# A pair of linear attentions on one core: the places of all jobs written anew

## The chip, the cores and the metric

The kernel runs on one core of a Trainium2 chip. The metric is the time of one execution on the device in microseconds (us). The core has five engines, each with its own stream of instructions, which it works off strictly in order: TensorE (PE, matmuls), VectorE (DVE), ScalarE (ACT), GpSimd (POOL) and SyncE (SP). SP and POOL also issue the DMA transfers, each on a queue of its own (q1 hardware for SP, q0 software for POOL). Engines wait for each other on semaphores.

## The reference, cut to what matters

```python
def _A_ref(x, wqkv, wo):                   # x [1, 2048, 640], wqkv [640, 1920], wo [640, 640]
    qkv = (x @ wqkv).reshape(B, S, 3, 32, 20)       # then q, k, v per head
    phi = lambda t: jnp.where(t > 0, t + 1, jnp.exp(t)) + 1e-6
    pq, pk = phi(q), phi(k)
    kv  = jnp.einsum("bhsd,bhse->bhde", pk, v)
    z   = jnp.einsum("bhsd->bhd", pk)
    num = jnp.einsum("bhqd,bhde->bhqe", pq, kv)
    den = jnp.einsum("bhqd,bhd->bhq", pq, z)[..., None] + 1e-6
    return (num / den) [heads joined] @ wo
```

There are two such blocks, A and B, each with an x and weights of its own, and the results are put side by side. All is float32.

## The kernel before, in words

**Arithmetic.** Each float32 operand is split into a high part (rounded to the format that TensorE takes, written by ACT) and a low part (source less high part, by DVE), and each product is made of three matmuls, high by high, high by low, low by high. In the names of tiles, `h` and `l` at the end are the two parts. The products with wk, wq and the output matrix use a scheme with seven products in place of eight (`STEPS`, `product`), which needs sums and differences of quarter tiles of x: for pair p of 128-row tiles, `A1`, `A2`, `A5` are pieces of x (tiles `kah`, `kal`) and `S1`, `S3` the sums (`sx`, rounded to `ksh`, `ksl`). Seven products of a pair are called n = 0 to 6; between them ACT copies partial results out of PSUM (`c0` after product 0, `c2` after 2, `c4` after 4, `c5` after 5), and DVE adds others (`q3`, `q4`, `q6`). Products 2, 4 and 5 use again the PSUM bank that c0, c2, c4 empty, so they can't start before these copies are done.

**The k half** (from the start to about 285 us): for both inputs, tile by tile, pk = phi(x wk), then G = pk^T x, and from G with wv the state kv. Tile n of 32 (16 per input) gives `xt` (transposed tile, for the products), `xn` (plain tile, for G; split by `nh` on ACT, L484, and `nl` on DVE), `ek`, `ko`, `pkh`, `pkl` (phi and its two parts: jobs `exp`, `relu`, `mix`, `ph`, `pl`), and a store `zs` that adds phi to an accumulator in DRAM. The tiles are in groups of four, i = 0 to 7; a group's products of two pairs come first, with the sums of G (`psg`) of the group before between them.

**The form of x from the k half.** The low parts and the sums that the k half makes of the last groups' x are stored to DRAM (`xd` by SP, jobs `st`; `sd` by POOL, jobs `ss`, for pairs 10 to 13, two sums S1 and S3 with a high and a low part each) and loaded again for q.

**The q half** (from about 285 us): per block of 512 rows u, pq = phi(x wq), its denominator, the division, and the output with a matrix that holds kv and wo. The last two blocks (6 and 7, the "joint q") are computed together with the seven-product scheme on the forms of x that the k half stored (`qpair`, slots `r` 0 to 45): `load_xs` loads plain x (512-byte runs), `xs_lo` and `x5_lo` load low parts from `xd`, `load_s` loads sums from `sd`. Meanwhile block 5 finishes: four `gather` DMAs (`rd<-da`) bring 1/denominator, DVE divides (L1036), ACT and DVE split the result. Then come three output blocks (`outmm`), whose products also wait for copies out of PSUM (`o<-pa`, `o<-pe`).

**What sets the order.** Nothing is scheduled by a tool: the order of every engine's stream is the order in which the program issues it. In the k half, PE's work is a list of steps, and all other work is a list of jobs, each at a float place near a step. Three tables at the top of the file shift them: `MOVED` shifts steps, `SHIFT` shifts jobs (`SHIFT.get(name, 0)` is added to the job's place), and the sorted list is then issued. In the q half jobs hang at slots of `line`, one per matmul group, and `AT` moves a job by so many slots:

```python
spot = round((place[spot] if isinstance(spot, tuple) else spot) + SHIFT.get(name, 0), 2)   # job
steps.sort(key=lambda w: w[0] + MOVED.get(w[2], 0))                                        # arrange
slot = line[line.index(slot) + AT.get((f.__name__,) + a, 0)]                               # at
```

Since each engine works in order, a job that waits holds up all that stands behind it on the same engine. SP and POOL too: an issue that waits for a buffer or for data holds up the issues behind it. Buffers come from pools with a fixed number per tag (the tiles `xt` and `xn` share five, the sums have two), so the order also decides which buffer a tile gets and what it must wait for.

## Time and profile before

| | |
|---|---|
| median of three runs | 570.23 us (570.09 to 571.23) |
| the profiled execution | 570.55 us, span 568.8 us |
| PE | 560.7 us busy (99%), 3219 instructions |
| DVE | 432.4 us (76%), 739 |
| ACT | 335.4 us (59%), 627 |
| POOL | 102.5 us (18%), 167 |
| DMA | 136.19 MB, mean 239 GB/s; q1 (SP) 48.6% and q0 (POOL) 29.1% of 16 engines' span |

A row of a timeline gives start, length, engine, line, operation, output and inputs, and in brackets the idle time before it with what ended it. `<-` stands between output and inputs; buffer numbers are left out. A row of the windows gives the stretch, its length, then the busy time and count of PE, of PE's weight loads, DVE, ACT and POOL, then the granted clock of PE (1.00 is full), the share of the 16 DMA engines that was busy, and GB/s. A matmul's start follows that of the one ahead in 0.15 us (320 columns) or 0.23 us (512 columns), though each row is 0.31 or 0.39 us long, since they are pipelined.

### The profile page before, as it was taken

How to read it: one execution, taken by the hardware profiler on the slowest of the kernel's cores; microseconds unless marked ns; L12 is line 12 of the kernel's file. 1: busy time of each engine (PE TensorE's matmuls, PEld its weight loads, DVE VectorE, ACT ScalarE, POOL GpSimd, SP SyncE). 2: the span in 40 equal slices, each digit the busy share in tenths (PEclk: the TensorE clock that was granted, in tenths of full speed). 3: DMA queues.
4: the chain of work that ended last, by engine and by line, in shares of the span. 5: the costliest groups of instructions: out<-in, count | busy, mean ns of one | idle time of the engine just before them, and what ended most of it. 6: DMA issues, size and time to landing. Idle time of an engine off the chain costs nothing.

```text
span 568.8 us, 9177 instructions
## 1 busy us (share of the span) xinstructions
PE 560.7 (99%) x3219; PEld 511.1 (90%) x3219; DVE 432.4 (76%) x739; ACT 335.4 (59%) x627; POOL 102.5 (18%) x167
## 2 busy tenths in 40 slices
PE   9999999999999989999999999999999999999997
PEld 7989999898989978989888899898989989779997
DVE  5889798886585867878754896968969496769881
ACT  5874667662775856565835774645537273574441
POOL 0111122311014323243010103111012211100110
PEclk9999999999999999999999999999999999999999
DMA  8869789999898897999997995847567897940322
GB/s 262 245 163 247 182 234 312 270 322 355 296 249 233 209 303 139 355 280 235 317 323 266 324 308 171 283 142 248 168 227 243 276 369 226 321 155 20 112 94 92
DMA packets 85174, 136.19 MB, mean 239 GB/s; under 512 B 10312, under 2 KB 45512, under 8 KB 85128
## 3 DMA queue, kind: packets, MB, share of 16 engines
q1 hardware_dynamic: 70600, 88.90, 48.6%
q0 software_dynamic: 14240, 46.48, 29.1%
q8 instruction: 25, 0.41, 0.3%
q10 hardware_dynamic: 288, 0.23, 0.1%
q14 instruction: 21, 0.17, 0.1%
HBM read 78.34 MB, written 54.09 MB: 233 GB/s over the span
## 4 chain that ended last, share of the span: by engine, by line
PE 91%; DMA 3%; DVE 2%; ACT 2%; issue 1%; SPq 0%; DVEq 0%; ACTq 0%
PE pa L337 20%; PE pe L337 10%; PE psg L163 8%; PE psg L164 8%; PE psg L162 8%; PE psb L337 7%; PE psq L162 6%; PE psq L164 6%; PE psq L163 6%; PE psk L605 5%; DMA xn<-in_B_x 2%; PE pskv L787 2%; PE pa L1230 1%; DMA x<-xd 1%; DMA x<-in_B_xt 1%; PE pe L1230 1%
## 5 line engine op out<-in xcount | busy, mean ns | idle before, releaser
L162 PE MATMUL psg<-pkh,xnh 128*128 128x512 f32 x160 | 62.7, 392 | 0.0
L164 PE MATMUL psg<-pkh,xnl 128*128 128x512 f32 x160 | 62.7, 392 | 0.0
L163 PE MATMUL psg<-pkl,xnh 128*128 128x512 f32 x160 | 62.6, 392 | 0.0
L162 PE MATMUL psq<-xqh,wqh 128*128 128x512 f32 x150 | 58.9, 393 | 0.0
L164 PE MATMUL psq<-xqh,wql 128*128 128x512 f32 x150 | 58.5, 390 | 0.0
L163 PE MATMUL psq<-xql,wqh 128*128 128x512 f32 x150 | 58.4, 390 | 0.0
L341 ACT ACTIVATE o<-pa 128x320 f32<-128x320 f32 x64 | 27.7, 437 | 51.7 <-PE pa L337 51.6
L572 POOL DMA_DIRECT2D zd<-ek x30 | 26.3, 876 | 125.7 <-DVE ek L564 44.8
L341 ACT ACTIVATE ko<-pa 128x320 f32<-128x320 f32 x52 | 22.4, 434 | 38.9 <-PE pa L337 38.6
L164 PEld LDWEIGHTS psg<-pkh,xnl 128*128 128x128 f32 x160 | 30.0, 188 | 6.5
L163 PEld LDWEIGHTS psg<-pkl,xnh 128*128 128x128 f32 x160 | 30.1, 188 | 5.5 <-DVE pkl L580 0.3
L162 PEld LDWEIGHTS psg<-pkh,xnh 128*128 128x128 f32 x160 | 30.1, 188 | 5.2
L1036 DVE SCALAR_TENSOR_TENSOR pq<-pq,rd 128x1280 f32<-128x1280 f32 x16 | 23.1, 1480 | 13.9 <-DMA rd<-da 13.9
L164 PEld LDWEIGHTS psq<-xqh,wql 128*128 128x128 f32 x150 | 28.2, 188 | 6.0
L163 PEld LDWEIGHTS psq<-xql,wqh 128*128 128x128 f32 x150 | 28.2, 188 | 5.4
L162 PEld LDWEIGHTS psq<-xqh,wqh 128*128 128x128 f32 x150 | 28.2, 188 | 5.4
L576 ACT ACTIVATE pkh<-ek,epst 128x640 fp32r<-128x640 f32 x32 | 25.9, 823 | 10.7 <-DVE ek L564 10.6
L650 DVE TENSOR_TENSOR gacc<-psg,gacc 128x512 f32<-128x512 f32 (+2 forms) x42 | 25.6, 628 | 8.5 <-PE psg L164 8.4
L564 DVE SCALAR_TENSOR_TENSOR ek<-ek,ko 128x640 f32<-128x640 f32 x32 | 26.2, 820 | 6.3 <-ACT ko L561 4.0
L155 ACT ACTIVATE dah<-pq 128x1024 fp32r<-128x1024 f32 (+2 forms) x24 | 17.7, 773 | 22.6 <-DVE pq L1036 22.6
L433 ACT ACTIVATE ksh<-sx 128x512 fp32r<-128x512 f32 x26 | 16.3, 629 | 24.6 <-DVE sx L451 24.5
L580 DVE SCALAR_TENSOR_TENSOR pkl<-ek,pkh 128x640 fp32r<-128x640 f32 x32 | 25.9, 820 | 5.6 <-ACT pkh L576 5.6
(289 smaller groups left out, 1793.7 us busy)
## 6 DMA issues: line engine op xcount, KB each, us to landing
zd<-ek POOLq DMA_DIRECT2D x32, 320.0 KB, 5.4
out<-o POOLq DMA_DIRECT2D x28, 320.0 KB, 3.2
xql<-xd SPq DMA_DIRECT2D x24, 256.0 KB, 4.6
xt<-in_B_xt_tiles SPq DMA_DIRECT2D x16, 320.0 KB, 4.7
xn<-in_B_x SPq DMA_DIRECT2D x16, 320.0 KB, 5.7
xqs<-in_A_xt SPq DMA_DIRECT2D x20, 256.0 KB, 6.1
fdmh<-fsh POOLq DMA_DIRECT2D x14, 320.0 KB, 4.6
fdml<-fsl POOLq DMA_DIRECT2D x14, 320.0 KB, 5.2
```

Source lines behind the costliest of these rows:

```text
L162: nc.tensor.matmul(o, whi, xhi, start=first, stop=False)
L163: nc.tensor.matmul(o, whi, xlo, start=False, stop=False)
L164: nc.tensor.matmul(o, wlo, xhi, start=False, stop=last)
L337: nc.tensor.matmul(o, x, y, start=start and m == r == 0, stop=m == len(terms) - 1 and r == 2, skip_group_check=True)
L341: nc.scalar.activation(x, y, AF.Copy)
L564: nc.vector.scalar_tensor_tensor(ek[n], ek[n], 1.0, rk[n], op0=OP.min, op1=OP.add)
L572: nc.gpsimd.dma_start(zacc[b], e, accum_op=OP.add)
L576: nc.scalar.activation(pk[n][0], ek[n], AF.Identity, bias=epst)
L580: nc.vector.scalar_tensor_tensor(lo, ek[n], EPS, f32(hi), op0=OP.add, op1=OP.subtract)
L605: nc.tensor.matmul(kps["c", n][h], plain_x(n, c)[i], plain_w(c)[j][:, h * HF:(h + 1) * HF], start=(c == 0 and i == j == 0), stop=(c == NC ...
L650: nc.vector.tensor_tensor(o, x, o, op=OP.add)
L1036: nc.vector.scalar_tensor_tensor(p, p, EPS, r, op0=OP.add, op1=OP.mult)
```

## The change

Only the three tables are other ones; from `GROUPS` on the file is the same, 49 lines higher. Every engine has the same work to do, except that the first sum of block 7's denominator on ACT and the last on DVE take each other's chunk. A part of the diff, with the entries that the text below touches:

```diff
-SHIFT = {
-    ('exp', 22): 1.7, ('n', 23): 2.26, ('nh', 20): 3.26, ('nh', 23): 2.58, ('ph', 20): 3.48,
...
-    ('t', 23): 1.5, ('t', 24): 0.99, ('t', 25): 3.77, ('zl',): 0.73, ('zs', 22): 1.61,
...
+SHIFT = {('exp', 22): 1.03, ('n', 23): 2.21, ('nh', 20): 2.26, ('nh', 23): 1.82, ('ph', 20): 2.55,
...
+ ('t', 23): 5.71, ('t', 24): -0.57, ('t', 25): 2.91, ('t', 27): 1.04, ('zo',): -4.16, ('zl',): 0.73, ('zs', 22): 1.61,
+ ('ss', 11, 0, 0): 0, ('ss', 11, 0, 1): -1.81, ('ss', 11, 1, 0): 4, ('ss', 11, 1, 1): 4,
+ ('ss', 12, 0, 0): 3, ('ss', 12, 0, 1): 2.56, ('ss', 12, 1, 0): 8, ('ss', 12, 1, 1): 8}
...
-MOVED = {('G', 2, 5): 2.0, ('G', 6, 0): 4.0, ('H', 3, 0, 0): 3.5, ('H', 7, 2, 2): 1.5, ('c', 2, 3): -2.5, ('p', 14, 2): -2.0,
+MOVED = {('G', 2, 5): 2.0, ('G', 6, 0): 4.0, ('G', 6, 1): 1.5, ('H', 3, 0, 0): 3.5, ('H', 7, 2, 2): 1.5, ('c', 2, 3): -2.5,
+    ('p', 11, 6): 1, ('p', 14, 0): -1.5, ('p', 14, 2): -2.0, ('p', 7, 3): 1,
...
-AT = {('a_split', 7, 0): 4, ('d_split', 7, 0): 4, ('d_split', 7, 1): 2, ('load_xs', '11', 0): -9, ('load_xs', '12', 1): 2,
+AT = {('a_split', 7, 0): 6, ('acc7', 7, 0): 6, ('d_split', 7, 0): 5, ('d_split', 7, 1): 1, ('load_xs', '11', 0): -19,
+    ('load_xs', '22', 1): 2, ('mix7', 7, 0): -2, ('split_acc', 6): -1, ('x5_lo', 0): -3, ('xs_lo', '22', 0): 3,
+    ('xs_lo', '22', 1): 2,
```

The table `SHIFT` has some 330 entries, of which about a third have another value. What this does to the streams is seen in their order, here at three places.

SP at 195 to 212 us of the k half of input B. In a row stand the instruction's number, its line (49 lower in the change) and the transfer; `xt` and `xn` are tiles of x, `zs<-zd` the load of the sum over phi, `xd<-kal` a store of a low part. Before:

```order
112 L410 DMA xt<-in_B_xt_tiles 128x640
113 L240 DMA xd_2085<-kal 128x128
114 L731 DMA zs<-zd_295 128x640
115 L410 DMA xt<-in_B_xt_tiles 128x640
116 L410 DMA xn<-in_B_x 128x640
117 L410 DMA xt<-in_B_xt_tiles 128x640
118 L410 DMA xn<-in_B_x 128x640
```

and now:

```order
111 L361 DMA xt<-in_B_xt_tiles 128x640
112 L682 DMA zs<-zd_295 128x640
113 L191 DMA xd_2084<-kal 128x128
114 L361 DMA xn<-in_B_x 128x640
115 L361 DMA xt<-in_B_xt_tiles 128x640 x2
116 L361 DMA xn<-in_B_x 128x640
```

The `xn` of row 116 before (tile 23) now stands ahead of the `xt` of row 115 before (tile 27), and takes another buffer: before it waited for the subtraction of tile 22 on DVE, now for no engine. Tile 27 now follows tile 28, whose issue waits for that subtraction. On POOL at the same time six stores `sd` were issued one after the other (pairs 11 and 12, the second sums of pair 12 last); now four of them are, and the second sums of pair 12 come two `zs` stores later.

ACT at 202 to 212 us: phi of tiles 23 and 22 (`ek`, `ko`, `pkh`), the rounding of x tile 23 (`xnh`), and the copies `ko<-pa` of pair 12's products 2 and 4. Before:

```order
221 L341 ACTIVATE ko<-pa 128x320
222 L484 ACTIVATE xnh<-xn 128x640
223 L576 ACTIVATE pkh<-ek,epst 128x640
224 L552 ACTIVATE ek<-ko 128x640
225 L561 ACTIVATE ko<-ko 128x640
226 L341 ACTIVATE ko<-pa 128x320
```

and now:

```order
228 L435 ACTIVATE xnh<-xn 128x640
229 L292 ACTIVATE ko<-pa 128x320
230 L503 ACTIVATE ek<-ko 128x640
231 L512 ACTIVATE ko<-ko 128x640
232 L527 ACTIVATE pkh<-ek,epst 128x640
233 L292 ACTIVATE ko<-pa 128x320
```

The copy of product 2 (221 before, 229 now) stands behind the rounding of x tile 23 instead of ahead of it; between the two copies the order of three others is changed.

SP in the joint q part, about 488 to 499 us (`xql<-xd` low parts of x, `xs` plain x, `xql<-sd` low parts of sums, `x_5...<-xd` the low part of the fifth chunk). Before:

```order
248 L1160 DMA xql<-xd_2085 128x512 x2
249 L1139 DMA xs<-in_B_xt 128x4x128 x2
250 L1165 DMA xql<-sd_2182 128x512
251 L1176 DMA x_5769<-xd_2085 128x512
252 L1165 DMA xql<-sd_2182 128x512
253 L1160 DMA xql<-xd_2085 128x512 x2
254 L1176 DMA x_5809<-xd_2085 128x512
```

and now:

```order
244 L1111 DMA xql<-xd_2084 128x512 x2
245 L1090 DMA xs<-in_B_xt 128x4x128
246 L1127 DMA x_5750<-xd_2084 128x512
247 L1090 DMA xs<-in_B_xt 128x4x128
248 L1116 DMA xql<-sd_2220 128x512 x2
249 L1127 DMA x_5803<-xd_2084 128x512
250 L1111 DMA xql<-xd_2084 128x512 x2
```

The low part of the fifth chunk, which waits for DVE to free its buffer, now stands ahead of the second `xs` and of both `xql<-sd`. A little earlier on the same queue, the second load of x for the fourth form (`load_xs '12' 1`) stands ahead of the four gathers of block 5 instead of behind them. At the end, on ACT, the rounding `dah<-pq` of block 7 stands behind two copies `o<-pa` instead of ahead of them.

## The prediction

> **What bounds the kernel now.** I read the page's head first, then what TensorE (PE) waited for.

> ```profile
> span 568.8 us, 9177 instructions
> ```
> ```profile
> PE pa L337 <- ACT ko L341: 2.4, 1, 2.4
> PE psi L1349 <- PEq L1870: 0.8, 1, 0.8
> PE pe L337 <- DVE o L344: 0.5, 1, 0.5
> PE psb L1230 <- DMA x<-xd: 0.4, 1, 0.4
> PE pa L337 <- ACT o L341: 0.2, 1, 0.2
> PE pa L1230 <- DMA xql<-sd: 0.2, 1, 0.2
> ```

> The columns are microseconds in total, times, longest. PE is the bound, and the same matmuls run in both kernels, so a new order can only remove or add stalls of PE. After the start-up row (psi) the list holds five waits, 3.7 us together, and the one at line 337 is two thirds of it. Its stretch, with the granted clock (the number ahead of the DMA share, which is ahead of GB/s):

> ```profile
> 210.00:215.00 5.00, 3.94 (x16) 3.94 (x17) 2.81 (x5) 3.46 (x6) 0.67 (x1) 0.66 0.73 195
> ```

> A mean clock of 0.66 over 5 us is (1 - 0.66) x 5 = 1.7 us of full-speed work lost. So the stall costs 2.4 + 1.7 = 4.1 us. PE's own rows there:

> ```profile
> 205.78 0.31 PE L337 MATMUL pa<-wfh,ksh 128*128 128x320 f32 x1
> ...
> 211.06 0.63 PE L337 MATMUL pa<-wfh,kah 128*128 128x320 f32 x1 [2.41 <-ACT ko L341]
> ```

> The row at 205.78 opens product 4 of pair 12, the row at 211.06 its product 5; without the stall the latter would have begun at 211.06 - 2.41 = 208.65. What held ScalarE (ACT) is in the chain of waits (start, length, what):

> ```profile
> 198.63 9.18 DMA xn<-in_B_x
> ...
> 208.57 0.72 ACT pkh L576
> 209.28 0.64 ACT ek L552
> ...
> 209.94 0.74 ACT ko L561
> 210.68 0.34 ACT ko L341
> ```

> and between the load and the row at 208.57 stands the second row of ACT's timeline:

> ```profile
> 204.60 0.44 ACT L341 ACTIVATE ko<-pa 128x320 f32<-128x320 f32 x1 [0.22 <-PE pa L337]
> 207.83 0.74 ACT L484 ACTIVATE xnh<-xn 128x640 fp32r<-128x640 f32 x1 [2.79 <-DMA xn<-in_B_x]
> ```

> ACT copies product 2 of pair 12 out of PSUM at 204.60, then stands 2.79 us at the rounding of x tile 23, which landed only at 207.81. Three operations and the copy of product 4 are queued behind it, and PE needs that copy's bank. A late load is the cause, ACT's fixed order carries it to PE.

> **The change at 196 to 212 us, the main term.** Before, SyncE (SP) issues in this order:

> ```profile
> 196.91 0.50 SPq L410 DMA_DIRECT2D xt<-in_B_xt_tiles  x1
> 198.63 0.33 SPq L410 DMA_DIRECT2D xn<-in_B_x  x1
> ```

> and for the first of the two the rows by tile give

> ```profile
> DMA to landing us min/median/max: 8.9/8.9/8.9
> ```

> So the transposed tile 27 landed at 196.91 + 8.9 = 205.8 and x tile 23, next on the queue, 2.0 us later, at 198.63 + 9.18 = 207.8. The change puts tile 23 ahead of tile 27 and gives it a buffer that is free, so that it no longer waits for a subtraction on DVE. It has 128x640 elements, like the tile whose place it takes. Call its landing L. I take L = 205.8. Not earlier, because the four stores by GpSimd that still lie ahead of that time fill the other queue as before; the two that go to a later place (the second sums of pair 12) stood behind the others.

> ACT's order changes as well, and this speaks against the change: the copy of product 2 is now queued behind the rounding of tile 23. Product 4 starts when that copy is done. From the chain's steps the copy ends at L + 0.74 + 0.34, and with 0.06 between the links PE is released at L + 1.14. Product 4 was due at 205.78, so PE stands for S = L + 1.14 - 205.78 = L - 204.64. At L = 205.8 this is 1.2 us. The second stall then vanishes: the copy of product 4 comes 0.64 + 0.74 + 0.72 + 0.34 = 2.44 us after the first copy, at about L + 3.6, and product 5 is due at 208.65 + S = L + 4.0. Both move with L, so for every late L there is one stall, not two. Tile 27 comes later by two places, at 2.0 us each 4 us, at about 209.8; its first readers are the sums of pair 13, behind all of pair 12's products that are left, and these hide it. The moved stores hold only buffers that pair 14 takes again, later still. If this cover were gone, a wait there could be no longer than those 4 us.

> The price runs from both sides. With L up to 204.6 there is no stall: 4.1 us gained. With L still 207.8 the stall is 3.2 us plus the clock, 4.9 in all, a loss of 0.8. With 205.8 it is 1.2 us against 4.1: **2.9 us gained**, if the clock stays up.

> Whether it stays up no row decides: a gap of 2.41 us was followed by the low clock, those of up to 0.5 us were not, and 1.2 lies between, nearer to the gaps that cost nothing. So I take 0, with 1.7 as the other end. [...]

> **The change in the joint q part, 477 to 505 us.** The rows of SP, of VectorE (DVE) and of the chain:

> ```profile
> 479.85 2.60 SPq L1029 DMA_DIRECT2D rd<-da  x4
> 482.49 0.59 SPq L1139 DMA_DIRECT2D xs<-in_B_xt  x1
> ...
> 490.76 1.20 SPq L1165 DMA_DIRECT2D xql<-sd  x1
> 494.42 0.34 SPq L1176 DMA_DIRECT2D x<-xd  x1
> ```
> ```profile
> 486.19 2.89 DVE L1036 SCALAR_TENSOR_TENSOR pq<-pq,rd 128x1280 f32<-128x1280 f32 x2 [2.82 <-DMA rd<-da]
> ```
> ```profile
> 490.09 0.58 ACT pq L341
> ...
> 494.42 4.90 DMA x<-xd
> ```

> and PE's:

> ```profile
> 491.09 0.40 PE L1230 MATMUL pa<-xql,wfh 128*128 128x512 f32 x1
> 491.33 0.40 PE L1230 MATMUL pa<-xqh,wfl 128*128 128x512 f32 x1
> 491.86 0.50 PE L1230 MATMUL pa<-xqh,wfh 128*128 128x512 f32 x1
> 492.56 0.50 PE L1230 MATMUL pa<-xql,wfh 128*128 128x512 f32 x1 [0.20 <-DMA xql<-sd]
> ...
> 501.57 0.39 PE L1230 MATMUL pa<-xql,wfh 128*128 128x512 f32 x1
> ```

> Matmuls of this shape follow each other every 0.24 us (491.09, 491.33), so 491.86 is 0.29 late and 492.56 is 0.46 late: both wait for the loaded sums of the second product.

> (a) One load of x (the xs row at 482.49) goes ahead of the four gathers at 479.85. What is issued behind it, the loaded sums too, finds a queue that is shorter by it. At the rate of this stretch,

> ```profile
> 480.00:485.00 5.00, 5.00 (x31) 4.60 (x30) 1.48 (x4) 1.07 (x2) 1.83 (x4) 1.00 0.92 287
> ```

> 256 KB at 287 GB/s is 0.9 us. This covers both delays: 0.75 us gained, or 0 if those loads keep their landings.

> (b) The same load now lies in front of the gathers, and DVE waits for these (2.82 us idle, until 486.19). A delay of d passes through the division, ACT's rounding and the copy at 490.09 (ended 490.67) to the first matmul of the group, one ahead of the row at 491.09, at 490.85: 0.2 us of room. The share of 0.92 in that row says that the queues had some room, so d lies between 0 and the whole 0.9; the middle, 0.5, costs 0.3 us.

> (c) The low half of x's fifth chunk (x<-xd) is issued when DVE is done, at 494.42 as before, but ahead of two loads that lay before it. At 0.9 us for each of the two it comes 1.8 us earlier, and the wait of 0.4 us in the list (psb <- DMA x) ends.

> (d) Those two loads (one of x, and the low half of the third product's sums) now stand on SP behind its wait until 494.4. The latter was issued at 490.76 and took

> ```profile
> DMA to landing us min/median/max: 7.8/7.8/7.8
> ```

> to land at 498.6; PE reads it at 501.57. Issued at 495.4 with a flight of 4.9, like the x<-xd row beside it, it lands at 500.3, and PE, 0.9 us ahead by then, wants it at 500.7: no cost, with 0.4 us of room. With its old flight it would land at 503.2, 2.5 late.

> The sum is -0.75 + 0.3 - 0.4, about **0.9 us gained**, with ends at 1.2 gained (d = 0) and 2.0 lost (d = 0.9, (d) late, (a) and (c) gained).

> **The change at the end.** Two copies out of PSUM go ahead of a rounding on ACT that stands before the wait listed as 0.2 us (pa <- ACT o). This wait ends: **0.2 gained**. The rounding comes later by two copies (0.44 us each, by the copy at 204.60) and what they wait for; the products of the block before the last cover it, and if they don't, it costs up to 1 us. The listed 0.5 us at pe on DVE stays: the order of its producers is not changed.

> All other moves (some of one to eight places on each engine, and two swaps of products on PE) lie where no wait of PE is listed; I cost them at nothing, because PE's queue of ready matmuls covers them, and give them half a microsecond either way.

> **Sum.** 2.9 + 0.9 + 0.2 = 4.0. The profiled execution took 570.55 us (span 568.8 and 1.75 around it), which would become 566.5; the median of the runs is 0.3 lower, 570.23, and so becomes **566.2**.

> **Rivals.** A difference of 0.2%, 1.1 us, is about what can be told from no change.

> 1. The forecast: L near 205.8, one short stall, the clock stays up. 566.2, own range 565.2 to 567.5. Chance 0.46.
> 2. No stall at all: with two stores fewer on the other queue L comes to 204.6. 570.23 - 4.1 - 0.9 - 0.2 = 565.0. For it: fewer bytes; against it: these bytes lay behind. Chance 0.10.
> 3. The clock falls after 1.2 us as it did after 2.41: 566.2 + 1.7 = 567.9. [...] Chance 0.16.
> 4. The loads behind SP's wait in the joint part come 2.5 us late: 566.2 + 2.5 = 568.7. For it: the flight of 7.8; against: that was flown with a full queue ahead. Chance 0.08.
> 5. Tile 23 is not earlier: the queue's bandwidth, not its place, sets L. Because the copy of product 2 is now behind it, the stretch costs L - 204.64 + 1.7 against 4.1. At L = 207.8: 0.8 lost, 1.1 gained elsewhere, 569.9, no change. Chance 0.10. From L = 208.1 the kernel is slower than before, from 209.3 by over 0.2%; one place on the queue further, at 209.8, it is 571.9. For it: both tiles took 9 us, though issued 1.7 apart; against: no transfer of its size has moved ahead of tile 23. Chance 0.10, which also has to hold a new wait elsewhere of that size.

> **How the numbers follow.** Faster: 0.46 + 0.10 + 0.16 + 0.08 = 0.80. Same 0.10, slower 0.10. The range leaves out the slower cases and a little below rival 2: 564.6 to 570.4.

> **What would show it.** Right: the wait pa <- ACT ko is about 1.2 us at product 4 of pair 12 (near 206), none at product 5, the clock row of 210:215 reads 1.00, xn lands near 205.8 after an issue near 196.9; the rows pa <- DMA xql and psb <- DMA x are gone. Wrong: a landing at 207 or later, a granted clock below 1 behind 206, DVE's wait for rd longer than 2.82 with a PE stall at about 490, or a wait for xql<-sd near 501.

## The result and the profile after

The changed kernel takes 568.13 us (median of 21 runs, 565.68 to 572.94); the kernel before, on the same chip, 571.73 us (21 runs, 569.3 to 573.29). The ratio is 0.995, with a 95% interval of 0.9928 to 0.9971: faster by 0.5%. On the median that the prediction started from, 570.23 us, that is 567.4 us (566.1 to 568.6); predicted were 566.2. The 21 times of the changed kernel lie in two groups: 12 with a full mean granted clock (565.7 to 569.2 us), and 9 with a mean of 0.993 to 0.997 (569.7 to 572.9 us).

The profiled execution took 567.16 us, its span is 565.4 us, 3.4 less than before. Lines are now 49 lower: the copies out of PSUM are L292, the rounding of a tile of x L435, a product's matmul L288, one of the joint q part L1181. The list of waits, PE's part of it in full (us in total, times, longest):

```profile
PE psk L556 <- ACT kah L106: 0.9, 1, 0.9
PE pa L1181 <- ACT pq L292: 0.8, 1, 0.8
PE psi L1300 <- PEq L1821: 0.8, 1, 0.8
PE pe L288 <- DVE o L295: 0.4, 1, 0.4
```

The longest wait of before, PE's on ACT's copy `ko` at 2.4 us, is gone, and so are pa <- DMA xql, psb <- DMA x and pa <- ACT o. New is pa <- ACT pq in the joint q part (and one of 0.9 us at the start, at 8.5 us, where no other profile has more than 0.2). The timeline at the place of the main term, SP and ACT:

```profile
195.01 0.36 SPq L682 DMA_DIRECT2D zs<-zd  x1
195.43 0.42 SPq L191 DMA_DIRECT2D xd<-kal  x1
195.90 0.42 SPq L361 DMA_DIRECT2D xn<-in_B_x  x1
...
204.61 0.72 ACT L435 ACTIVATE xnh<-xn 128x640 fp32r<-128x640 f32 x1
205.24 0.41 ACT L292 ACTIVATE ko<-pa 128x320 f32<-128x320 f32 x1
```

The rows of the tile `xn` for that load, and the windows (columns as explained before; the clock is the third number from the end):

```profile
DMA to landing us min/median/max: 7.1/7.1/7.1
```
```profile
205.00:210.00 5.00, 5.00 (x30) 4.52 (x29) 4.21 (x7) 4.31 (x8) 0.90 (x1) 1.00 0.96 286
210.00:215.00 5.00, 5.00 (x27) 4.37 (x27) 2.84 (x5) 3.80 (x6) 2.43 (x3) 1.00 0.69 116
```

Tile 23 was issued at 195.90 and landed 7.1 us later, at 203.0. The rounding at 204.61 has no idle time in brackets: ACT had other work until then, and the data were there. PE was busy for all 10 us at full clock. So the whole stall of 4.1 us (gap and clock) is gone, not 2.9 of it.

The joint q part, DVE's division and PE's first matmul behind it, and under them the rows of the tile `rd`:

```profile
483.92 2.90 DVE L987 SCALAR_TENSOR_TENSOR pq<-pq,rd 128x1280 f32<-128x1280 f32 x2 [3.91 <-DMA rd<-da]
...
488.44 0.50 PE L1181 MATMUL pa<-xqh,wfh 128*128 128x512 f32 x1 [0.79 <-ACT pq L292]
```
```profile
DMA to landing us min/median/max: 4.8/5.0/5.2
```

DVE waited 3.91 us for the gathers (2.82 before) and PE stood for 0.8 us behind it.

**Lost time by stretch.** For all profiles of this study I took PE's matmuls in order and summed by how much each start came later than is usual behind a matmul of the form ahead of it (the median distance of the two starts), where that is over 0.06 us. The sum holds the gaps and what a low clock costs. In us:

| kernel | ratio to before (95%) | pair 12, 200 to 222 | pairs 13 and 14, 222 to 250 | joint q, 478 to 506 | end, 525 to 556 |
|---|---|---|---|---|---|
| before | 571.73 us | 4.2 | 0.0 | 1.6 | 1.4 |
| changed | 0.9950 (0.9928 to 0.9971) | 0.0 | 0.5 | 1.8 | 1.2 |
| e1 changed, again | 0.9968 (0.9935 to 1.0001) | 0.0 | 0.0 | 1.7 | 0.9 |
| e2 changed, copy first | 0.9958 (0.9930 to 0.9986) | 0.0 | 2.0 | 4.5 | 1.0 |
| e3 before, tile 23 first | 1.0008 (0.9985 to 1.0031) | 0.4 | 4.2 | 2.3 | 1.6 |
| e4 before, rounding first | 0.9999 (0.9974 to 1.0025) | 2.5 | 1.9 | 1.1 | 0.9 |
| e5 before, tiles 23 and 25 | 0.9975 (0.9960 to 0.9991) | 0.7 | 2.3 | 1.7 | 0.9 |
| e6 changed, tile 25 back | 0.9939 (0.9917 to 0.9960) | 0.0 | 3.2 | 0.4 | 0.5 |
| e7 changed, gathers first | 0.9935 (0.9910 to 0.9960) | 0.0 | 1.7 | 2.5 | 1.2 |
| e8 before, load first | 1.0011 (0.9995 to 1.0028) | 4.0 | 0.3 | 1.4 | 1.7 |
| e9 changed, form roundings later | 0.9939 (0.9916 to 0.9962) | 0.0 | 2.4 | 1.9 | 0.7 |
| e10 changed, both loads of x first | 0.9934 (0.9910 to 0.9958) | 0.0 | 4.3 | 0.7 | 0.9 |
| e11 e9 + e10 + copy first | 0.9915 (0.9885 to 0.9945) | 0.0 | 0.1 | 2.0 | 1.2 |
| e12 changed, stores back | 0.9987 (0.9953 to 1.0021) | 0.0 | 3.8 | 5.4 | 0.5 |

The stretches are one execution each, the ratios a median over some 6 to 21. The table says two things at once. Where tile 23 stands early, at most 0.7 us is lost at pair 12, instead of 2.5 to 4.2. And the two columns beside it vary from 0 to 4.3 and from 0.4 to 5.4 us, even between kernels whose order there is the same: that is where the gain went in part.

### The profile page after: what moved, and what is told of

Same layout as the page of the kernel before. It is cut to its first block, busy times and chain, and to the rows that moved or that the text cites. A ratio compares the mean times of both kernels' runs of the same rounds, so it can differ in the third digit from the quotient of the medians.

```text
span 565.4 us, 9168 instructions
## 1 busy us (share of the span) xinstructions
PE 558.8 (99%) x3219; PEld 509.0 (90%) x3219; DVE 432.8 (77%) x739; ACT 334.2 (59%) x627; POOL 102.3 (18%) x167
## 4 chain that ended last, share of the span: by engine, by line
PE 89%; DMA 5%; DVE 3%; ACT 1%; issue 1%; SPq 1%; POOL 0%; DVEq 0%; ACTq 0%; POOLq 0%
PE pa L288 20%; PE pe L288 10%; PE psg L114 7%; PE psg L115 7%; PE psg L113 7%; PE psb L288 7%; PE psq L113 6%; PE psq L115 6%; PE psq L114 6%; PE psk L556 4%; PE pskv L738 2%; PE pa L1181 2%; DMA zd<-ek 1%; DMA wst<-in_A_wk 1%; DMA sd<-ksh 1%
## 5 line engine op out<-in xcount | busy, mean ns | idle before, releaser
L292 ACT ACTIVATE o<-pa 128x320 f32<-128x320 f32 x64 | 27.8, 438 | 55.2 <-PE pa L288 55.2
L292 ACT ACTIVATE ko<-pa 128x320 f32<-128x320 f32 x52 | 22.5, 432 | 38.1 <-PE pa L288 37.9
```

The lines of the kernel that those rows point to most:

```text
L292: nc.scalar.activation(x, y, AF.Copy)
```

## The experiments

### The place of tile 23 and what stands beside it

**e1, the changed kernel itself again**, to see how far one execution can be trusted.

> The changed kernel as it is, run again. In its 21 timed runs two groups showed: 13 at a mean clock of 1.000 (565.7 to 569.2 us) and 8 at 0.993 to 0.997 (569.7 to 572.9 us); 0.003 of 566 us is 1.7 us, one stretch at half clock. Theory A: in the second group x tile 23 landed late (206 or later), so that the copy of product 2 of pair 12, queued behind its rounding, stopped PE by L - 204.64 and the clock fell. Then about a third of the runs lies in the second group again, and a profile that falls there shows a stall at product 4 of pair 12. Theory B: the second group comes from another stall (the start, where the profile has a gap of 0.87 us at 8.5, or the gathers of the joint part, 0.79 us at 488); then a profile of that group shows pair 12 without a stall.

It took 569.49 us (12 runs), a ratio of 0.9968 whose interval just reaches 1. In 8 of the runs the mean clock was below 1 (of the 21 runs of the result it was 9, not the 8 that the expectation counts). The profile, with a span of 563.4 us the shortest of all, is one of the other four and has no stall at all in pairs 12 to 14, so it can't tell theory A from B. One and the same program profiled at 565.4 and 563.4 us: a difference of 2 us between two single profiles proves nothing here, and only the place of a wait and what ended it do, the better the more profiles agree.

**e2, ACT's copy of product 2 ahead of the rounding of tile 23 again.**

```diff
-('nh', 23): 1.82
+('nh', 23): 2.05
```

> The changed kernel with one entry other: the copy of product 2 of pair 12 stands ahead of the rounding of x tile 23 on ACT, as it did before. Theory A: a late tile 23 now costs L + 3.25 - 208.65 instead of L - 204.64, 0.8 us less, and nothing up to L = 205.4 instead of 204.6. The share of runs at 0.997 falls from a third to a tenth or none, and the median by 0.5 to 1.5 us against e1. Theory B: share and median as in e1.

Ratio 0.9958, like the changed kernel's: the swapped order of copy and rounding, which the prediction held against the change, costs nothing that can be told once the data are early. Theory A (a late tile 23 is what lowers the clock in some runs) expected a tenth of such runs or none; it was 5 of 12, though the copy no longer stood behind the tile. The profiles in which the clock did fall with these tables (e10 and e12) show it behind gaps at 234 and 495 us.

**e3, the kernel before with tile 23 alone at the earlier place, and e4, with the rounding alone ahead of the copy.**

```diff
 e3: -('n', 23): 2.26     +('n', 23): 1.9
 e4: -('nh', 23): 2.58    +('nh', 23): 1.9
```

> The kernel before with one entry other: on SP's queue x tile 23 stands ahead of the transposed tile 27 (which now waits for the subtraction). ACT, DVE, POOL and PE as before. Theory of the place on the queue: tile 23 lands about 2.0 us earlier, at 205.8, the copy of product 4 is done at 209.05 and the stall at product 5 falls from 2.41 to 0.4 us, the half clock goes: 3.7 us faster than before. If it lands at 203 as in the changed kernel: no stall, 4.1 faster. Theory of the bandwidth: it still lands near 207.8, and the time is that of before.

> The kernel before with one entry other: on ACT the rounding of x tile 23 stands ahead of the copy of product 2, as in the changed kernel; all transfers as before. By the prediction's formula PE stands for L - 204.64, 3.2 us at L = 207.8, at product 4 instead of 2.41 us at product 5: 0.8 us slower than before. Rival: the order of these two does not matter, the stall stays 2.4 us in all and the time is that of before.

In e3 tile 23 was issued at 196.0 and landed 8.3 us later, at 204.3, instead of 207.8. One entry of SP's order brought that, so it is the place on the queue that made the tile late, and the theory of the bandwidth fell. The kernel took 570.91 us, ratio 1.0008: **no gain, though the stall of pair 12 is gone** (0.4 us lost there instead of 4.2). None of the theories had this. The loss came back 25 us later:

```profile
227.17 0.44 ACT L341 ACTIVATE ko<-pa 128x320 f32<-128x320 f32 x1 [2.75 <-PE pa L337]
...
233.04 0.74 ACT L909 ACTIVATE fsh<-wst 128x640 fp32r<-128x640 f32 x1 [4.26 <-DVE wst L884]
233.69 0.42 ACT L341 ACTIVATE ko<-pa 128x320 f32<-128x320 f32 x1
...
235.14 0.74 ACT L484 ACTIVATE xnh<-xn 128x640 fp32r<-128x640 f32 x1 [1.03 <-DMA xn<-in_B_x]
...
234.16 0.42 PE L337 MATMUL pa<-wfh,ksh 128*128 128x320 f32 x1 [2.19 <-ACT ko L341]
```

ACT stands 4.26 us in front of a rounding `fsh` that waits for DVE, and the copy that product 4 of pair 13 needs stands behind it (a second gap, of 1.48 us at 238.5, follows). In e4 (571.53 us, ratio 0.9999, not the expected 0.8 us slower) the rounding waits for the late tile with the copy behind it: one gap of 2.23 us at 208.0. The tile landed at 206.89 here, for which the prediction's L - 204.64 gives 2.25: its formula for the copy behind the rounding fits. The clock stays up in the stretch behind it, unlike in e8, which has the order of before here and a gap of 2.26 us. The windows at 210 of e4 and of e8:

```profile
210.00:215.00 5.00, 5.00 (x30) 4.56 (x29) 3.14 (x5) 3.61 (x8) 0.02 (x1) 1.00 0.65 172
```
```profile
210.00:215.00 5.00, 4.68 (x20) 4.64 (x21) 2.86 (x5) 2.79 (x5) 0.89 (x1) 0.66 0.59 159
```

**e5, the kernel before with tiles 23 and 25 earlier** (both as in the change), and **e6, the changed kernel with tile 25 at its old place.**

```diff
 e5: before   -('n', 23): 2.26, ('n', 25): 3.9    +('n', 23): 1.9, ('n', 25): 0.28
 e6: changed  -('n', 25): 0.28                    +('n', 25): 3.9
```

> The kernel before with two entries other: x tile 23 ahead of transposed tile 27 as in the last such run, and x tile 25 directly behind tile 26 on SP's queue, ahead of three transfers, as in the changed kernel. With tile 23 alone the stall at 211 went, but stalls of 2.2 us at 234 and 1.5 us at 238 came in its place, behind x tiles 26 and 25. Theory A (the same wait one group later, set by the place of tile 25 on the queue): the stall at 238 goes, that at 234 is smaller, and the kernel is 2 to 3.5 us faster than before. Theory B (the transfers as a whole are late there, whatever their order): the stall at 238 stays or moves to another load, and the time stays within 0.8 us of that of before.

> The changed kernel with x tile 25 put back to its place before, behind two stores and one load. Theory A: PE stalls 1.5 to 3 us at about 238, and the kernel loses this against the changed kernel: it stands 0 to 1 us below before. Theory B: no stall there beyond the 0.3 us that the changed kernel has, same time as the changed kernel.

e5 took 569.3 us, ratio 0.9975: with tile 25 earlier too, about half of the change's gain is there, and 2.3 us instead of 4.2 are lost in pairs 13 and 14. e6 took 567.06 us, ratio 0.9939, no slower than the change: there tile 25 is not what ACT waits for. What it waits for is the rounding `fsh` again (a gap of 2.95 us at 234.9). In e5, with tile 25 early, ACT stands 3.20 us at the same rounding. So tile 25 is one of several loads that stand ahead of the same copies, and having one of them early leaves the others to be waited for.

### Why pairs 13 and 14 take back part of the gain

Four profiles have the changed kernel's order up to 250 us (changed, e1, e7, e10), and e12 has it on all engines but GpSimd. Product 4 of pair 13 needs a copy that stands on ACT behind `fsh`, the rounding of a sum that DVE forms (L834) of `wst`, which SP loads from `md` when GpSimd's store of `md` has landed. In each fence is a copy whose time PE sets, the sum's first subtraction, and PE's wait, where there is one; first e1, then the changed kernel, e7, and e10:

```profile
226.83 0.44 ACT L292 ACTIVATE ko<-pa 128x320 f32<-128x320 f32 x1 [4.32 <-PE pa L288]
227.90 0.49 DVE L834 TENSOR_TENSOR t<-wst 128x320 f32<-128x320 f32 x1 [0.65 <-DMA wst<-md]
```
```profile
227.89 0.44 ACT L292 ACTIVATE ko<-pa 128x320 f32<-128x320 f32 x1 [4.32 <-PE pa L288]
229.50 0.49 DVE L834 TENSOR_TENSOR t<-wst 128x320 f32<-128x320 f32 x1 [1.20 <-DMA sd<-ksh]
```
```profile
227.27 0.44 ACT L292 ACTIVATE ko<-pa 128x320 f32<-128x320 f32 x1 [4.32 <-PE pa L288]
230.22 0.49 DVE L834 TENSOR_TENSOR t<-wst 128x320 f32<-128x320 f32 x1 [2.54 <-DMA wst<-md]
233.53 0.42 PE L288 MATMUL pa<-wfh,ksh 128*128 128x320 f32 x1 [1.46 <-ACT ko L292]
```
```profile
226.90 0.44 ACT L292 ACTIVATE ko<-pa 128x320 f32<-128x320 f32 x1 [4.32 <-PE pa L288]
230.94 0.49 DVE L834 TENSOR_TENSOR t<-wst 128x320 f32<-128x320 f32 x1 [3.62 <-DMA wst<-md]
234.24 0.42 PE L288 MATMUL pa<-wfh,ksh 128*128 128x320 f32 x1 [2.54 <-ACT ko L292]
```

From copy to subtraction it is 1.07, 1.61, 2.95 and 4.04 us; PE's gap is 0, 0.1, 1.46 and 2.54. The gap is the difference less 1.5 us, or nothing where that is below 0, in all four (in e6, 231.61 - 227.16 - 1.5 = 2.95, and in e2 230.42 - 227.54 - 1.5 = 1.38, both as measured). Nothing else is needed to explain it: PE waits as long as this sum is more than 1.5 us late. And the sum is late by the loads' doing: in each of these profiles the subtraction starts 0.12 or 0.13 us after the second of the three loads of `wst` has landed (in the changed kernel too, at 229.38, though the trace puts that wait down to a store). This is shown.

**e9, two of ACT's roundings `fsh` moved behind the copies.**

```diff
+('fh', 'm', 0, 0): 3.05, ('fh', 'm', 0, 2): 1.1
```

> The changed kernel with two of ACT's roundings of a form's sum (fsh, for the q half of block 0) moved behind the copies c0 14 and c2 13. Theory G (the gain of tile 23 is partly given back one group later, because ACT stands at a rounding that waits for loads, in front of the copy that product 4 of pair 13 needs): the PE stall at 230 to 240 us, 0 to 3 us in the changed kernel's profiles, ends (below 0.5 us), ACT's idle time in front of these roundings holds up no copy, and the median falls by 0.5 to 1.5 us beside the changed kernel's (about 0.3% below its ratio of 0.995). Rival H (the products there wait for the transfers themselves, whatever ACT's order): a stall of 1 to 3 us stays or shows at the next reader of these roundings or loads, and the ratio stays 0.995 within 0.002. The joint part is not touched: a stall of 0.8 to 3 us behind the gathers may show in either case.

It took 568.05 us, ratio 0.9939. Theory G holds only in part: the wait behind `fsh` is gone, but in its profile PE stands 1.64 us at 236.3, since now the roundings of tiles of x are the first on ACT that wait for loads (rival H):

```profile
232.68 0.74 ACT L435 ACTIVATE xnh<-xn 128x640 fp32r<-128x640 f32 x1 [1.04 <-DMA xn<-in_B_x]
...
235.21 0.74 ACT L435 ACTIVATE xnh<-xn 128x640 fp32r<-128x640 f32 x1 [0.54 <-DMA xn<-in_B_x]
235.85 0.42 ACT L292 ACTIVATE ko<-pa 128x320 f32<-128x320 f32 x1
```

The expected fall of 0.5 to 1.5 us against the changed kernel's ratio lies within the intervals (0.9939 against 0.9950) and is not shown.

**e12, GpSimd's stores of pairs 11 and 12 at their old places**, six in a burst again. The orders of the other engines stay.

```diff
-('ss', 11, 0, 0): 0, ('ss', 11, 0, 1): -1.81, ('ss', 11, 1, 0): 4, ('ss', 11, 1, 1): 4,
-('ss', 12, 0, 0): 3, ('ss', 12, 0, 1): 2.56, ('ss', 12, 1, 0): 8, ('ss', 12, 1, 1): 8
```

> The changed kernel with GpSimd's stores of pairs 11 and 12 (sd) put back to their places of before: six in one burst near 196 us again, so that the two of pair 12's second sums no longer come behind two stores of phi. Nothing else is moved: the orders of SP, ACT and DVE are the changed kernel's. Theory P (the place on SP's queue brought tile 23 earlier, the two stores fewer only about 0.8 us of it): tile 23 takes 8.3 to 8.4 us as with six stores in the two kernels of before that have it in the earlier place, instead of 6.7 to 8.5 (median 7.6 in eight profiles with four stores); it lands at 203.5 to 204.3, still under the bound of 204.6, so no stall over 0.3 us at 204 to 212 us, and the ratio is the changed kernel's, 0.994 to 0.997. Rival Q (the moved stores are what brought it earlier): a flight of 9 us or more, landing behind 204.6, a stall of 0.5 to 2 us there, ratio 0.997 to 0.999. Rival R (the moved stores lie in the way of the loads and form sums at 220 to 235 us and cause the stall there): it is below 0.5 us in this kernel, and the ratio falls to 0.992 to 0.994.

It took 570.69 us, ratio 0.9987 (0.9953 to 1.0021): **without the moved stores no gain can be told**. But the interval overlaps those of the changed kernel and of e1, and e1's reaches 1 as well. None of the three theories had this time. Tile 23 took 7.3 us, as with four stores and less than theory P's 8.3, landed at 203.1, and the stall of pair 12 stayed away: rival Q fell, and what theory P says of the place on the queue held. The stall at 230 us did not end: rival R fell. The rows of e12, GpSimd, ACT and PE:

```profile
199.45 1.59 POOL L207 DMA_DIRECT2D sd<-ksl  x1
205.70 0.90 POOL L523 DMA_DIRECT2D zd<-ek  x1 [4.66 <-DVE ek L515]
...
212.50 0.74 ACT L503 ACTIVATE ek<-ko 128x640 f32<-128x640 f32 x1 [1.13 <-DMA zd<-ek]
...
219.30 0.87 POOL L824 DMA_DIRECT2D md<-mev  x1
...
234.56 0.42 PE L288 MATMUL pa<-wfh,ksh 128*128 128x320 f32 x1 [2.03 <-ACT ko L292]
```

and ACT's row of the changed kernel to compare:

```profile
212.17 0.74 ACT L503 ACTIVATE ek<-ko 128x640 f32<-128x640 f32 x1 [0.64 <-DVE ko L295]
```

Behind six stores the store of phi (`zd<-ek`, 205.70) holds its buffer so long that ACT's next exponential waits 1.13 us for it. In all eight other profiles with the changed kernel's tables this exponential waits 0.64 us, and for DVE. e3 and e5, the two profiles of the tables of before that have tile 23 early, have six stores too, and there it waits 2.57 and 1.54 us, for this store. So three profiles against eight show the wait. From there it goes on: phi, its store at 218.71, and in order behind it the store of `md` at 219.30, 8.4 us ahead of the copy that PE sets (227.72). In all eight that distance is 9.1. Six stores thus cost the chain of `md` and `wst` 0.7 us of its lead, 25 us on and by way of a buffer.

What this costs PE is not shown. The gap of 2.03 us is again the sum's lateness, 231.25 - 227.72 - 1.5, but the four profiles of the changed order have gaps of 0 to 2.54 us with four stores. And the largest loss of e12's profile, 5.4 us, lies in the joint part, where its order is the changed kernel's.

### The joint q part

**e8, the kernel before with the load of x ahead of the gathers**, as in the change, and **e7, the changed kernel with the gathers ahead of it again.**

```diff
 e8: before   -('load_xs', '12', 1): 2
 e7: changed  +('load_xs', '12', 1): 2
```

> The kernel before with the same load of x ahead of the gathers: the prediction's steps (a) and (b) alone. By the prediction: 0.75 us gained at the loaded sums and 0.3 lost at the gathers, 0.45 us faster. By theory A of the run before it: gathers of 4.8 us and more, a PE stall of 0.8 us or more at about 491, the two stalls at the loaded sums covered by it, so 0 to 2 us slower. By theory B: gathers stay at 3.6 us, and it is 0.75 us faster.

> The changed kernel with one load of x put back behind the four gathers of block 5. In three profiles of the changed order the gathers took 4.8 to 6.6 us (median) instead of 3.0 to 3.6, and PE stalled 0.8, 0.8 and 3.1 us for what hangs on them. Theory A (the load ahead of the gathers is what makes them late): that stall goes, the 0.3 and 0.5 us stalls at the loaded sums come back, and the kernel is 0.3 to 2 us faster than the changed one, and the fastest so far. Theory B (the gathers are late because PE and the output stores reach this place sooner): gathers and stall stay, and the time does not move.

e8 took 571.85 us, ratio 1.0011: step (a) gains nothing that can be told. In its profile the gathers landed as early as before and the wait for the first loaded sum was gone, but PE lost 1.4 us in the joint part instead of 1.6. e7 took 566.95 us, ratio 0.9935, and PE still stood 1.31 us behind the division. So the load ahead of the gathers did not make them late in the kernel before, and without it they are late in the changed one all the same: theory A of e7 and step (b)'s reason are not what decides.

What makes them late goes back a block. Rows of four profiles (e6, changed, e7, e12), the division of the block before and the first of four issues of `da<-acc`, which spreads the denominator and stands on SP ahead of the loads of x and the gathers:

```profile
451.59 1.49 DVE L987 SCALAR_TENSOR_TENSOR pq<-pq,rd 128x1280 f32<-128x1280 f32 x1 [3.80 <-DMA rd<-da]
...
470.90 2.57 SPq L966 DMA_DIRECT2D da<-acc  x4
```
```profile
450.71 1.49 DVE L987 SCALAR_TENSOR_TENSOR pq<-pq,rd 128x1280 f32<-128x1280 f32 x1 [4.88 <-DMA rd<-da]
...
470.02 2.57 SPq L966 DMA_DIRECT2D da<-acc  x4
```
```profile
452.60 1.49 DVE L987 SCALAR_TENSOR_TENSOR pq<-pq,rd 128x1280 f32<-128x1280 f32 x1 [6.19 <-DMA rd<-da]
...
471.91 2.57 SPq L966 DMA_DIRECT2D da<-acc  x4
```
```profile
455.34 1.49 DVE L987 SCALAR_TENSOR_TENSOR pq<-pq,rd 128x1280 f32<-128x1280 f32 x1 [6.37 <-DMA rd<-da]
...
474.64 2.57 SPq L966 DMA_DIRECT2D da<-acc  x4
494.57 0.75 PE L1181 MATMUL pa<-xqh,wfh 128*128 128x512 f32 x1 [3.10 <-ACT pq L292]
```

From division to spread it is 19.3 us in each of them (470.90 - 451.59, and so on) and in all others of the changed tables. DVE has one wait on the way, 1.23 us for ACT in each, so nothing there takes up a delay. Against PE's own pace (its first matmul `ps<-xqh,wqh` of the joint part) the spread comes 10.4 us ahead in e6, 9.3 in the changed kernel, 8.0 in e7, e2 and e12. PE's gap behind the next division follows in that order, 0, 0.8, then 1.3, 3.1 and 3.1: the later the spread, the later SP issues the loads of x behind it, and the longer they are in flight beside the gathers. The last load of x issued ahead of the gathers landed 0.5, 1.9, 2.7, 3.3 and 3.3 us after the last gather was issued. This also tells what the load put ahead does: at the same spread of 8.0, e7, which has it behind the gathers, lost 1.3 us and the other two 3.1. So it adds to the delay where the spread is late; in e8 the spread came 11.7 us ahead, and that run could not show it. Late gathers of one block thus make the next block's late.

**e10, both loads of x of the fourth form ahead of the spread.**

```diff
+('load_xs', '12', 0): -7, ('load_xs', '12', 1): -7
```

> The changed kernel with both loads of x of the fourth form (load_xs 12) issued before the spread of the denominator, seven slots earlier. Theory J (the four gathers are late when loads of x are still in flight as they are issued): the loads have landed by then, the gathers take at most 3.8 us instead of 4.5 to 5.5, DVE waits for rd under 3 us, no PE stall over 0.3 us at 484 to 493 us, about 1 us gained (ratio 0.993). Rival K (what SP issues late there is late because SP itself waits for buffers; loads put ahead make it wait longer): the spread is issued later relative to PE, the gathers land as late as now or later, PE stalls 1 to 3 us, ratio 0.995 to 1.000. The stretch at 195 to 240 us is the changed kernel's.

567.97 us, ratio 0.9934. Theory J holds in the profile: the spread was as late as in e7 (8.0 us ahead), and yet the last gather landed 3.6 us behind the mark instead of 5.0, DVE waited 3.05 us, and no gap behind the division is left (0.7 us lost in the joint part, the second lowest of the table).

```profile
486.16 2.90 DVE L987 SCALAR_TENSOR_TENSOR pq<-pq,rd 128x1280 f32<-128x1280 f32 x2 [3.05 <-DMA rd<-da]
...
492.13 0.50 PE L1181 MATMUL pa<-xql,wfh 128*128 128x512 f32 x1 [0.24 <-DMA xql<-sd]
```

The last load of x ahead of the gathers landed as the last gather was issued. So it is the loads of x still under way that hold the gathers, and a late spread is what leaves them under way; that an early load cures it rests on this profile and e11's. Rival K fell. That this profile is not faster as a whole is pairs 13 and 14 again (4.3 us).

**e11, e9, e10 and e2's order together.**

> The changed kernel with the roundings of the form's sum later, both loads of x of the fourth form earlier, and the copy of product 2 of pair 12 ahead of the rounding of tile 23 again. If theories G and J hold, no stall over 0.5 us is left between 200 and 500 us: profile span about 563 to 564 us, median 565 to 566 us, ratio 0.990 to 0.992. If H or K holds, one of these stalls stays, and the time is that of the changed kernel, 567 to 569.

565.81 us (6 runs), ratio 0.9915 (0.9885 to 0.9945): the lowest of all kernels here, 0.35% below the changed kernel's ratio, though the intervals overlap. Nothing is lost in pairs 12 to 14. In the joint part the gathers are early (DVE waits 2.62 us), but another edge shows: ACT's copy `pq<-pa` waits 1.2 us and PE 0.85. That copy takes the buffer of the last output blocks, and the store of the last of these landed 0.24 us ahead of it, 7.3 us after its issue instead of 5.1 to 6.9 in the other profiles of these tables. The trace's inferred releaser is another (PE), so this reading is argued from the times, not shown.

## Why the prediction was right, and where it was not

The time and the range held. By stretches the changed kernel's profile lost 3.7 us less than that of before (7.2 to 3.5 over the four of the table), where the prediction's sum was 4.0. The span fell by 3.4, since the start took 0.5 us longer in this profile, and the timed runs by 2.8 (1.6 to 4.1). That 3.7 and 4.0 agree is partly luck, since three terms missed and cancelled.

- **The main term** was right in its mechanism: tile 23's place on SP's queue decided the stall (e3), and the formula for the copy behind the rounding holds (e4). Its size was off: 4.1 us gained instead of 2.9. The step that failed is "I take L = 205.8. Not earlier, because the four stores by GpSimd ... fill the other queue as before". L was 203.0, below the bound of 204.6, so the outcome at this place was rival 2's, which had a chance of 0.10. The issue came 1.0 us earlier than the old tile 27's, and the flight was 7.1 us instead of 8.9. The two stores fewer are not needed for this (e12: 7.3 us with six). e3 and e5 had 8.3 and 8.4 at the same place in the order of before, which lies within the 7.1 to 8.5 of the four profiles of the changed order. What makes the flight vary stays open; in all nine profiles of the changed tables the tile landed at 202.0 to 203.9, ahead of 204.6.
- **The clock** was taken as "no row decides", which was true of the rows it had. It stayed up in the changed kernel's profile because no gap was left there. That the stall before costs 1.7 us of clock was read off one execution as if it came each time. It does not: of the 96 timed runs of the kernel before that were taken beside the experiments, 49 have a mean clock of 0.999 or 1.000. In about half the runs, then, it cost no clock, which is one reason why the timed gain is less than the profile's. Which gaps were followed by a low clock is in the last section.
- **"All other moves ... cost at nothing"** is the step that failed most. It was read off a list of PE's waits in which pairs 13 and 14 had none. But that was because PE came 4 us late there, and every load was in time: with the stall of 4.0 to 4.2 us (before, e8) 0.0 and 0.3 us were lost in these pairs, without it in e3 4.2. With the stall gone, PE comes early and the loads don't: 0.5 us lost in the changed kernel's profile, 0 to 4.3 in those with the same order there. The prediction's cover for the stores ("hold only buffers that pair 14 takes again") left out the phi stores that stand behind them on GpSimd (0.7 us of lead in e12; what PE pays for it is open).
- **Joint q:** (c) was right, 0.4 us: psb <- DMA x is gone in all profiles of the changed tables. (a) was mis-sized: 0.75 us by the sum, 0.2 in e8's profile and nothing in its time. (b) was mis-sized the other way: 0.3 us expected, 1.0 lost in the changed kernel's profile (by so much the start at 488.44 is later than usual), and mainly for another reason, the late spread, to which the load put ahead adds. (d) "no cost" had too little room: xql <- sd costs 0.1 to 0.6 us near 500 in four of the changed tables' profiles. The part as a whole lost 0.2 us instead of gaining 0.9.
- **The end** was right: pa <- ACT o is gone, pe <- DVE o is still there; 0.2 us gained.

So 4.0 predicted, plus 1.3 at pair 12, less 0.5 at pairs 13 and 14, less 1.1 in the joint part, makes the 3.7 found.

## What to carry to other kernels

When a stall of the bounding engine goes, what runs on transfers behind it, not on that engine's pace, can be later against it by as much, as at pairs 13 and 14 here: look in the next 30 us for an in-order engine that stands at such an operation with a copy behind it that the bounding engine needs, before the gain is booked. Measure lateness against a mark that the bounding engine sets, not on the clock of the trace; then a chain of fixed length (here 19.3 us from division to spread, or 1.5 us of room at a sum) shows at once. And where waits stand at the edge, compare the place of the waits in several profiles, not the length of two.

## What the runs showed of the hardware

```profile
231.82:235.23 3.41, 1.38 (x9) 1.12 (x9) 3.38 (x7) 2.85 (x6) 1.30 (x2) 1.00 1.06 354
235.23:238.64 3.41, 3.41 (x15) 3.41 (x14) 3.41 (x6) 1.63 (x3) 1.65 (x3) 0.50 1.04 411
```
```profile
232.26:235.67 3.41, 1.43 (x10) 1.43 (x11) 3.38 (x7) 3.10 (x6) 1.86 (x3) 1.00 1.05 379
235.67:239.09 3.42, 3.42 (x15) 3.42 (x14) 3.42 (x6) 1.06 (x2) 1.08 (x2) 0.50 0.98 329
```
```profile
487.50:490.92 3.42, 1.60 (x8) 0.98 (x6) 3.24 (x3) 0.35 (x1) 1.10 (x2) 1.00 1.05 353
490.92:494.33 3.41, 2.17 (x9) 1.60 (x10) 3.38 (x5) 3.41 (x6) 0.00 (x0) 1.00 0.97 326
```

The gap of 3.07 us in e2 lies across a border, with 1.82 us ahead of it and 1.25 behind, and costs only itself; the gap of 2.03 us in e12 lies within one stretch. The cost beside the gap was nearly the same each time: by the table of lost time 1.7 to 1.8 us (4.2 less 2.41 in before, 4.0 less 2.26 in e8, 3.8 less 2.03 in e12, 4.3 less 2.54 in e10), about half of the 3.41 us at a clock of 0.50. A mean clock of 0.997 in a timed run is about one such stretch (1.7 of 566 us); the profile of before, with one of them, has a mean of 0.997.

**Transfers of one order differed by up to 2.1 us from profile to profile.** In the four profiles of the changed kernel's order the median flight of the three loads of `wst` issued together was 5.2, 5.5, 6.1 and 7.3 us, tile 23's 7.1 to 8.5. PE lost 0 to 4.3 us in pairs 13 and 14 of these profiles, where it waits for such loads.
